# Two buffers for a tile's exponentials, one for the halves of z, in a fused attention and feed-forward kernel

## The chip, the cores and the metric

The kernel runs on one core of a Trainium2 chip. The metric is the device time of one execution in microseconds (us). Five engines work side by side, each through its own list of instructions in order: TensorE (PE in the profile; its weight loads are PEld), VectorE (DVE), ScalarE (ACT), GpSimd (POOL) and SyncE (SP), which here only issues DMAs. An instruction that waits holds up everything behind it on its engine, and a DMA that waits holds up the DMAs behind it on SP.

## The reference, cut to what matters

```python
k_p = k.reshape(B, H, Sp, 8, D).mean(axis=3)      # B = H = 8, S = 576, D = 64, Sp = 72
v_p = v.reshape(B, H, Sp, 8, D).mean(axis=3)
scores = scale * np.matmul(q, k_p.transpose(0, 1, 3, 2))
attn = np.exp(scores - np.max(scores, axis=-1, keepdims=True))
attn = attn / (np.sum(attn, axis=-1, keepdims=True) + 1e-09)
x = np.matmul(attn, v_p)                           # to (8, 576, 512)
xn = (x - mean(x)) / sqrt(var(x) + 1e-06) * g_ln
out = x + np.maximum(xn @ w_ch1, 0.0) @ w_ch2      # w_ch1: 512 x 2048, w_ch2: 2048 x 512
```

All inputs and the output are float32.

## The kernel before, in words

The 4608 tokens are cut into 36 tiles of 128 and 9 chunks of 4 tiles. Each tile passes two attention stages, each chunk one feed-forward stage. Values that need more than 16 bits are carried as two f16 parts, a high and a low one, and products are taken as three f16 matmuls.

**Scores and exponentials** (`stage_a`, token A; `scores` and `probs`). Four pairs of heads give scores in f32 into the PSUM tile `ps_s`, of which there is one (line 280). DVE takes the maximum (289) and writes the difference to `e` (290). ACT takes the exponential in place (299) and casts the high parts into `phl` (300, 303); POOL subtracts them from `e` for the low parts (307, 310). A DMA that transposes sends `phl` to `pt` (317). There are two `phl` tiles, taken in turn, and one `e`.

**Values and normalization** (`values`, token B). PE multiplies `pt` with the pooled v into `ps_x`, of which there is one (336, 337). DVE and ACT divide by the sum into `x` (340 to 357), DVE normalizes it to `z` (361 to 383), ACT casts the high part of z into the tile `hl` (387, called `zhl` in the code), POOL subtracts for the low part (388), and a transposing DMA sends `hl` to the chunk's `zT` (392). There is one `z`, and there are two `hl`.

**Feed-forward** (`ffn_in`, token I; `ffn_out`, token O). Line 411 multiplies w1 with `zT`, ACT and DVE write the result as two parts to a `ring` tile (419, 420), line 440 multiplies with w2, and DVE adds to `x` (450). A block of 512 columns is 12 matmuls in line 411, a tile of a half is 24 in line 440.

**Preparation.** k and v are loaded and pooled, mostly by POOL (216 to 232). The 16 weight blocks of 1 MB each are loaded as raw 64-bit words (155; the `raw` pool has two buffers), converted (`convert`: 164 and 176 on ACT, 167 and 168 on DVE), scaled and split in two (139 on ACT, 140 on DVE).

**What sets the order.** The string `START` lists the operations of chunks 0 and 1 with the loads, conversions and splits between them; a loop then interleaves chunk c with the attention stages of chunk c + 1. This is only the order in which the code is recorded. The framework's scheduler then orders each engine's list and decides when a tile of a pool is free, by a timing model of its own; a pool's number of buffers is one of its inputs. In `START` the first inputs of chunk 0 come as two halves of columns (`I.0.q.0`, `I.0.q.1`): the first half needs `zT` of tiles 0 and 1, the second that of tiles 2 and 3, and those of chunk 1 (`I.1.q`) need all of tiles 4 to 7.

Of the kernel before, what the change touches and what calls it, by code (L numbers as in the profile page):

```python
# [8 lines left out]
F32 = mybir.dt.float32  # L9
F16 = mybir.dt.float16  # L10
# [7 lines left out]
P = 128  # L18
B, H, S, D = 8, 8, 576, 64
POOL = 8  # L20
KV = S // POOL
KA, KR = 64, KV - 64
KB = KV + 2 * KR
DM = H * D
# [36 lines left out]
def attn_ffn_kernel(ctx: ExitStack, tc: tile.TileContext, qT, kT, v, g, w1, w2, out):  # L61
# [3 lines left out]
    wk1 = ctx.enter_context(tc.tile_pool(name="wk1", bufs=1))  # L65
    wk2 = ctx.enter_context(tc.tile_pool(name="wk2", bufs=2))
# [33 lines left out]
    def scalar_tile(name, n=1):  # L100
        return small.tile([P, n], F32, name=name)
# [155 lines left out]
    q_sb, E, PT, X, Z, zTs = {}, {}, {}, {}, {}, {}  # L257

    def segments(t):

        lo, res = t * P, []
        while lo < (t + 1) * P:
            b = lo // S
            hi = min((t + 1) * P, (b + 1) * S)
            res.append((slice(lo - t * P, hi - t * P), b))
            lo = hi
        return res
# [3 lines left out]
        nc.sync.dma_start(out=q_sb[t], in_=qT[t])  # L271

    def scores(t):
        E[t] = e = wk1.tile([P, H, KV], F32, name="e")
        q = q_sb.pop(t)
        mx = scalar_tile("mx", H)
        ps = ps_s.tile([P, 2, 512], F32, name="ps_s")
        for p in range(NPAIR):
            for r, b in segments(t):
                nc.tensor.matmul(  # L280
                    ps[r, p // 2, p % 2 * 2 * KV : (p % 2 + 1) * 2 * KV],
                    lhsT=q[:, p, r],
                    rhs=kblk[b % NKB][:, p, :],
                    start=True,
                    stop=True,
                )
        sc = ps[:, :, : 4 * KV].rearrange("p a (h k) -> p a h k", k=KV)
        mx = mx.rearrange("p (a h) -> p a h", a=2)
        nc.vector.tensor_reduce(out=mx, in_=sc, axis=AX.X, op=ALU.max)  # L289
        nc.vector.tensor_tensor(  # L290
            out=e.rearrange("p (a h) k -> p a h k", a=2),
            in0=sc,
            in1=mx.unsqueeze(3).broadcast_to([P, 2, 4, KV]),
            op=ALU.subtract,
        )
# [23 lines left out]
    def values(t):  # L319

        segs = segments(t)
        if len(segs) == 1:
            cv = CV[segs[0][1]]
        else:
            cv = scalar_tile("cvm")
            for r, b in segs:
                nc.vector.tensor_copy(out=cv[r], in_=CV[b][r])
        pt = PT.pop(t)
        sm, rs = scalar_tile("sm", H), scalar_tile("rs", H)
        X[t] = x = xres.tile([P, DM], F32, name="x")  # L330
        ps = ps_x.tile([P, 2, 512], F32, name="ps_x")
        px = ps[:, :, : H // 2 * (D + 1)].rearrange("p a (h d) -> p a h d", d=D + 1)
        for r, b in segs:
            for h in range(H):
                o = px[r, h // 4, h % 4]
                nc.tensor.matmul(o, lhsT=pt[:, h, r], rhs=VA[b][:, h, :], start=True, stop=False)  # L336
                nc.tensor.matmul(  # L337
                    o, lhsT=pt[:KB, H + h, r], rhs=VB[b][:, h, :], start=False, stop=True
                )
        nc.vector.tensor_scalar(  # L340
            out=sm.rearrange("p (a h) -> p a h", a=2),
            in0=px[:, :, :, D],
            scalar1=1e-9,
            scalar2=cv,
            op0=ALU.add,
            op1=ALU.mult,
        )
        nc.vector.reciprocal(out=rs, in_=sm)
        xh = x.rearrange("p (h d) -> p h d", d=D)
        nc.vector.tensor_tensor(  # L350
            out=xh[:, 0:4, :],
            in0=px[:, 0, :, 0:D],
            in1=rs[:, 0:4].unsqueeze(2).broadcast_to([P, 4, D]),
            op=ALU.mult,
        )
        for i in range(4):
            nc.scalar.activation(  # L357
                out=xh[:, 4 + i, :], in_=px[:, 1, i, 0:D], func=AF.Copy, scale=rs[:, 4 + i : 5 + i]
            )
        st, mv = scalar_tile("st", 6), scalar_tile("mv2", 2)  # L360
        nc.vector.bn_stats(out=st, in_=x)  # L361
        nc.vector.bn_aggr(out=mv, in_=st)
        ve, y, a = scalar_tile("ve"), scalar_tile("y"), scalar_tile("a")
        nc.vector.tensor_scalar(
            out=ve, in0=mv[:, 1:2], scalar1=1e-6, scalar2=Z_VAR, op0=ALU.add, op1=ALU.mult
        )
        nc.vector.tensor_scalar(
            out=y.bitcast(I32),
            in0=ve.bitcast(I32),
            scalar1=-0.5,  # L370
            scalar2=RSQRT_MAGIC,
            op0=ALU.mult,
            op1=ALU.add,
        )
        for _ in range(3):
            nc.vector.tensor_scalar(
                out=a, in0=y, scalar1=ve, scalar2=y, op0=ALU.mult, op1=ALU.mult
            )
            nc.vector.tensor_scalar(
                out=y, in0=a, scalar1=1.5, scalar2=y, op0=ALU.subtract, op1=ALU.mult  # L380
            )
        Z[t] = z = wk1.tile([P, DM], F32, name="z")
        nc.vector.tensor_scalar(  # L383
            out=z, in0=x, scalar1=mv[:, 0:1], scalar2=y, op0=ALU.subtract, op1=ALU.mult
        )
        zhl = wk2.tile([P, 2, DM], F16, name="hl")
        nc.scalar.copy(out=zhl[:, 0, :], in_=z)  # L387
        nc.gpsimd.tensor_tensor(out=zhl[:, 1, :], in0=z, in1=zhl[:, 0, :], op=ALU.subtract)  # L388
        c, tt = divmod(t, TPC)
        if tt == 0:  # L390
            zTs[c] = wk2.tile([P, 2 * NKT, CH], F16, name="zT")
        nc.sync.dma_start_transpose(
            out=zTs[c][:, :, tt * P : (tt + 1) * P], in_=zhl.rearrange("p a d -> p (a d)")
        )
# [62 lines left out]
    def stage_a(t):  # L457
        if t + 2 < NTT:
            load_q(t + 2)
        scores(t)  # L460
        probs(t)
# [53 lines left out]
    def out_half(c, h):  # L515
# [3 lines left out]
    ops = {  # L519
        "LD": first_loads, "K0": first_k, "V0": first_v, "R": load_raw,  # L520
        "Q": load_q, "A": stage_a, "B": values, "C": convert, "M1": max_w1, "M2": max_w2, "S": split_w,
        "I": in_quarter, "O": out_half, "HK": half_k, "HV": half_v,
    }
# [4 lines left out]
    for c in range(2, NRUN):  # L528
        units = []
        for h in range(2):  # L530
            units += [(ffn_in, c, f) for f in range(h * NFT // 2, (h + 1) * NFT // 2)]
            units += [(ffn_out, c, tt, h) for tt in range(TPC)]
        for u, (op, *args) in enumerate(units):
            if c + 1 < NRUN:
                if u in A_AT:
                    stage_a((c + 1) * TPC + A_AT.index(u))
                if u in B_AT:
                    t = (c + 1) * TPC + B_AT.index(u)
                    values(t)
                    b = t * P // S + 2  # L540
                    if b < B and (t + 1) * P >= (b - 1) * S:
                        prep_k(b)
                        prep_v(b)
            op(*args)
# [26 lines left out]
```

## Time and profile before

| | us |
|---|---|
| three runs | 899.89, 900.61, 900.71 |
| median | 900.61 |
| the profiled execution | 902.73 |
| its span in the profile | 900.6 |
| PE busy in the span | 830.0 (92%) |
| DVE, ACT, POOL busy | 427.9, 264.3, 261.8 |

The span runs from the first to the last recorded instruction of the profiled execution, which took 2.1 us more than its span and 2.1 us more than the median of the three runs. Matmuls overlap each other in the records, so a busy PE is not a PE at its peak. Times in the trace are counted from the start of the span.

### The profile page before, as it was taken

Reading aid. Unit: us, or ns where it says so; the run is one execution under the profiler, and the core shown is the slowest. Engines: PE = TensorE matmul, PEld = TensorE weight load, DVE = VectorE, ACT = ScalarE, POOL = GpSimd, SP = SyncE. Lnnn points to the kernel's source line nnn. Section 1 sums busy time; section 2 is a strip of 40 time slices with the busy share of each in tenths; the row PEclk is TensorE's granted clock in tenths of the full one; section 3 lists DMA queues with packets and bytes.
Section 4 is the critical chain, followed back from the end, with each engine's and each line's share of the span. In section 5 each row is a group of like instructions: output and inputs, shape, how many; then the busy total and the mean of one; then the engine's idle time right before and its main releaser. Section 6 shows DMA issues by size and latency. Waiting matters only on the chain.

```text
span 900.6 us, 11909 instructions
## 1 busy us (share of the span) xinstructions
PE 830.0 (92%) x4524; PEld 419.3 (47%) x4524; DVE 427.9 (48%) x986; ACT 264.3 (29%) x513; POOL 261.8 (29%) x414
## 2 busy tenths in 40 slices
PE   2246895999999999999999999999999999999998
PEld 1235743444444444454454544544544454444443
DVE  7687795335562643365335533653354335432121
ACT  2675673314131221233123312331232123211020
POOL 5684688205242150056002620230011002100000
PEclk9999996999999999999999999999999999999999
DMA  8989996102352322254223432332223121310001
GB/s 305 275 220 276 261 261 153 27 0 65 77 129 72 62 66 62 59 138 100 50 59 86 114 71 59 85 69 56 59 59 83 36 59 36 70 38 22 1 1 47
DMA packets 137289, 84.80 MB, mean 94 GB/s; under 512 B 116113, under 2 KB 117265, under 8 KB 135185
## 3 DMA queue, kind: packets, MB, share of 16 engines
q1 hardware_dynamic: 135696, 82.86, 36.1%
q10 hardware_dynamic: 1536, 1.20, 0.6%
q8 instruction: 35, 0.57, 0.3%
q14 instruction: 22, 0.17, 0.1%
HBM read 45.09 MB, written 9.44 MB: 61 GB/s over the span
## 4 chain that ended last, share of the span: by engine, by line
PE 80%; DMA 9%; POOL 5%; DVE 2%; ACT 1%; issue 1%; SPq 1%; ACTq 0%; POOLq 0%
PE ps_f L411 38%; PE ps_f L440 38%; DMA pt<-phl 3%; PE ps_s L280 2%; DMA kr<-in_kT_dram 2%; DMA q<-in_qT_dram 1%; PE ps_x L336 1%; PE ps_x L337 1%; POOL kr L216 1%; DMA raw<-in_w_dram 1%; DVE w L168 1%; DMA raw<-in_v_dram 1%; DMA va<-vh 1%; POOL vr L230 1%; POOL phl L307 1%
## 5 line engine op out<-in xcount | busy, mean ns | idle before, releaser
L411 PE MATMUL ps_f<-zT,w 128*128 128x512 f16 (+1 forms) x1824 | 387.9, 372 | 4.6 <-DMA zT<-hl 3.9
L440 PE MATMUL ps_f<-w,ring 128*128 128x512 f16 x1728 | 379.1, 379 | 0.0
L411 PEld LDWEIGHTS <-w 128*128 128x128 f16 x1824 | 179.4, 99 | 195.7 <-issue 5.3
L440 PEld LDWEIGHTS <-ring 128*128 128x128 f16 x1728 | 168.1, 98 | 199.3 <-issue 0.2
L419 ACT ACTIVATE ring<-ps_f 128x512 f16<-128x512 f32 (+1 forms) x152 | 86.9, 573 | 275.3 <-PE ps_f L411 256.5
L420 DVE SCALAR_TENSOR_TENSOR ring<-ps_f,ring 128x512 f16<-128x512 f32 (+1 forms) x152 | 99.9, 659 | 140.5 <-ACT ring L419 138.8
L450 DVE SCALAR_TENSOR_TENSOR x<-ps_f,c_out,x 128x512 f32<-128x512 f32 x72 | 53.9, 749 | 187.4 <-PE ps_f L440 187.4
L307 POOL TENSOR_TENSOR phl<-e,phl 128x512 f16<-128x512 f32 x36 | 43.8, 1216 | 261.3 <-ACT phl L300 248.7
L280 PE MATMUL ps_s<-kblk,q 128*128 128x144 f32 (+1 forms) x320 | 56.3, 342 | 44.4 <-issue 22.5
L388 POOL TENSOR_TENSOR hl<-z,hl 128x512 f16<-128x512 f32 x36 | 42.7, 1185 | 125.3 <-ACT hl L387 120.3
L280 PEld LDWEIGHTS ps_s<-kblk,q 128*128 128x128 f32 (+1 forms) x320 | 47.9, 215 | 53.0 <-issue 32.6
L299 ACT ACTIVATE e<-e 128x576 f32<-128x576 f32 x36 | 24.6, 683 | 163.6 <-DVE e L290 156.6
L357 ACT ACTIVATE x<-ps_x,rs 128x64 f32<-128x64 f32 x144 | 33.3, 313 | 74.5 <-DVE x L350 33.3
L230 POOL TENSOR_TENSOR vr<-vr 72x256 f32<-72x256 f32 x56 | 45.5, 819 | 26.7 <-DMA vr<-in_v_dram 26.3
L300 ACT CAST phl<-e 128x1024 f16<-128x1024 f32 x36 | 37.5, 1041 | 8.0 <-DMA pt<-phl 7.5
L387 ACT CAST hl<-z 128x512 f16<-128x512 f32 x36 | 22.2, 617 | 57.0 <-DVE z L383 55.4
L232 POOL TENSOR_TENSOR vp<-vr 72x64 f32<-72x64 f32 x56 | 21.8, 405 | 57.8 <-DVE vb L140 57.5
L336 PE MATMUL ps_x<-va,pt 128*128 128x65 f16 (+1 forms) x320 | 27.5, 200 | 9.7 <-DMA pt<-phl 6.4
L361 DVE BATCH_NORM_STATS2 st<-x 128x6 f32<-128x512 f32 x36 | 24.9, 691 | 24.2 <-ACT x L357 24.0
L216 POOL TENSOR_TENSOR kr<-kr 128x288 f32<-128x288 f32 x29 | 25.7, 892 | 26.8 <-DMA kr<-in_kT_dram 26.4
L289 DVE TENSOR_REDUCE mx<-ps_s 128x8 f32<-128x576 f32 x36 | 26.8, 745 | 9.2 <-PE ps_s L280 9.1
L220 POOL TENSOR_TENSOR kblk<-kr 64x72 f32<-64x72 f32 x58 | 21.7, 374 | 32.1 <-PE ps_s L280 29.2
(80 smaller groups left out, 474.7 us busy)
## 6 DMA issues: line engine op xcount, KB each, us to landing
raw<-in_w_dram SPq DMA_DIRECT2D x12, 1024.0 KB
q<-in_qT_dram SPq DMA_DIRECT2D x36, 256.0 KB
out_dram<-x SPq DMA_DIRECT2D x36, 256.0 KB
kr<-in_kT_dram SPq DMA_DIRECT2D x30, 288.0 KB
vr<-in_v_dram SPq DMA_DIRECT2D x56, 144.0 KB
ring<-in_w_dram SPq DMA_DIRECT2D x4, 1024.0 KB
raw<-in_v_dram SPq DMA_DIRECT2D x8, 144.0 KB
va<-vh ACTq DMA_DIRECT2D x16, 65.0 KB
```

The source lines that it names most:

```text
L216: eng.tensor_add(out=kr[:, 0:4, :], in0=kr[:, 0:4, :], in1=kr[:, 4:8, :])
L230: eng.tensor_add(out=vr[:, 0:4, :], in0=vr[:, 0:4, :], in1=vr[:, 4:8, :])
L280: nc.tensor.matmul(ps[r, p // 2, p % 2 * 2 * KV : (p % 2 + 1) * 2 * KV], lhsT=q[:, p, r], rhs=kblk[b % NKB][:, p, :], start=True, stop=True,)
L300: nc.scalar.copy(out=ph[:, :, :, 0:KA], in_=e[:, :, 0:KA].unsqueeze(1).broadcast_to([P, 2, H, KA]))
L307: nc.gpsimd.tensor_tensor(out=ph[:, 0, :, KA:P], in0=e[:, :, 0:KA], in1=ph[:, 0, :, 0:KA], op=ALU.subtract)
L336: nc.tensor.matmul(o, lhsT=pt[:, h, r], rhs=VA[b][:, h, :], start=True, stop=False)
L388: nc.gpsimd.tensor_tensor(out=zhl[:, 1, :], in0=z, in1=zhl[:, 0, :], op=ALU.subtract)
L411: nc.tensor.matmul(ps, lhsT=w[:, part, fs], rhs=zT[:, kz, cols], start=(n == 0), stop=(n == 3 * NKT - 1),)
L419: nc.scalar.activation(out=h[:, 0, i, cols], in_=ps, func=AF.Relu)
L420: nc.vector.scalar_tensor_tensor(out=h[:, 1, i, cols], in0=ps, scalar=0.0, in1=h[:, 0, i, cols], op0=ALU.max, op1=ALU.subtract,)
L440: nc.tensor.matmul(ps, lhsT=h[:, part, i, cols], rhs=w[:, wp, j], start=(n == 0), stop=(n == 3 * NFT // 2 - 1),)
L450: nc.vector.scalar_tensor_tensor(out=x, in0=ps, scalar=c_out[:, half : half + 1], in1=x, op0=ALU.mult, op1=ALU.add)
```

## The change

Two pools change hands. `e` comes from a pool of two buffers, so that the difference of the next tile can be written while the last reader of the tile before is not done. `hl` comes from a pool of one, so that the high part of the next z waits until the transposing DMA has read the one before.

```diff
     def scores(t):
-        E[t] = e = wk1.tile([P, H, KV], F32, name="e")
+        E[t] = e = wk2.tile([P, H, KV], F32, name="e")
...
-        zhl = wk2.tile([P, 2, DM], F16, name="hl")
+        zhl = wk1.tile([P, 2, DM], F16, name="hl")
         nc.scalar.copy(out=zhl[:, 0, :], in_=z)
         nc.gpsimd.tensor_tensor(out=zhl[:, 1, :], in0=z, in1=zhl[:, 0, :], op=ALU.subtract)
```

No instruction is added or taken away. The scheduler's order of chunks 0 and 1 is another one on every engine; from the inputs of chunk 2 on it differs in a few places, and from tile 16 on PE's list is the same.

First place: ACT, from the first conversions of w2 to the first values (`e_348` is tile 2, `e_388` tile 3, `x_223` the values of tile 0). Before:

```order
L139 ACTIVATE w1_88<-w1_88,gs_92 128x1024
L300 CAST phl0_104<-e_348 128x16x64
L303 CAST phl0_104<-e_348 128x8x16
L176 ACTIVATE raw_433,wm2_96<-w2_89 128x1024
L139 ACTIVATE w1_88<-w1_88,gs_92 128x1024
L357 ACTIVATE x_223<-ps_x_224,rs_222 128x64 x4
L299 ACTIVATE e_388<-e_388 128x576
L139 ACTIVATE w1_88<-w1_88,gs_92 128x1024
L300 CAST phl1_105<-e_388 128x16x64
```

After:

```order
L299 ACTIVATE e_388<-e_388 128x576
L176 ACTIVATE raw_404,wm2_96<-w2_89 128x1024
L164 ACTIVATE w2_89<-raw_433 128x1024
L139 ACTIVATE w1_88<-w1_88,gs_92 128x1024
L300 CAST phl0_104<-e_348 128x16x64
L303 CAST phl0_104<-e_348 128x8x16
L176 ACTIVATE raw_433,wm2_96<-w2_89 128x1024
L139 ACTIVATE w1_88<-w1_88,gs_92 128x1024
L300 CAST phl1_105<-e_388 128x16x64
```

The exponential of tile 3 has moved ahead of the casts of tile 2, which it could not do with one `e`, and its casts ahead of the values of tile 0.

Second place: SP, around the transposing DMAs of tile 3's `hl` (`hl_550`) and of tile 6's exponentials (`pt_910`); `pt_1042` is tile 7, `raw_1076` and `raw_1078` are the last two blocks of w1, `raw_1551` and `raw_1555` blocks 5 and 6 of w2. Before:

```order
L271 DMA q_1766<-in_qT_dram 128x512
L155 DMA raw_1070<-in_w1_dram 128x2048
L392 DMA_TRANSPOSE zT_268<-hl_550 128x8x128
L155 DMA raw_1076<-in_w1_dram 128x2048
L211 DMA kr_1695<-in_kT_dram 128x576
L317 DMA_TRANSPOSE pt_910<-phl0_104 128x16x128
L317 DMA_TRANSPOSE pt_1042<-phl1_105 128x16x128
L155 DMA raw_1078<-in_w1_dram 128x2048
```

After:

```order
L155 DMA raw_1078<-in_w1_dram 128x2048
L271 DMA q_1828<-in_qT_dram 128x512
L211 DMA kr_1971<-in_kT_dram 128x576
L155 DMA raw_1551<-in_w2_dram 128x2048
L317 DMA_TRANSPOSE pt_910<-phl0_104 128x16x128
L392 DMA_TRANSPOSE zT_268<-hl_550 128x8x128
L317 DMA_TRANSPOSE pt_1042<-phl1_105 128x16x128
L155 DMA raw_1555<-in_w2_dram 128x2048
```

Two more weight blocks (and three pieces of k, three of v and one q, counted from the start) now stand ahead of `pt_910`, and tile 3's `hl` stands behind it.

Third place: PE, where the inputs of chunk 1 begin (`ps_f_1299`, line 411). `ps_x_1704` are the values of tile 8, `ps_s_2506` and `ps_s_2665` the scores of tiles 12 and 13, `ps_f_1268` the last outputs of chunk 0. Before:

```order
L337 MATMUL ps_x_1704<-vb_586,pt_1640 128x65
L280 MATMUL ps_s_2506<-kblk0_102,q_1828 128x144 x4
L280 MATMUL ps_s_2665<-kblk0_102,q_2263 64x144
L280 MATMUL ps_s_2665<-kblk1_103,q_2263 64x144
L411 LDWEIGHTS w1_88
L411 MATMUL ps_f_1299<-zT_777,w1_88 128x512
```

After:

```order
L440 LDWEIGHTS ring_783
L440 MATMUL ps_f_1268<-w2_89,ring_783 128x512
L411 LDWEIGHTS w1_88
L411 MATMUL ps_f_1299<-zT_777,w1_88 128x512
L411 LDWEIGHTS w1_88
```

Before, the values of tile 8 and the scores of tiles 12 and 13 (the two rows of `ps_s_2665` four times over) stood between the last outputs of chunk 0 and the inputs of chunk 1. Now nothing does: tiles 8 and 12 have moved in among the outputs of chunk 0, tile 13 behind the inputs of chunk 1. Further up, the rest of the scores of tile 9, the scores of tile 10 and the values of tile 6 have moved ahead of the second half of columns of chunk 0; before, the list came to that half straight after the values of tile 5. The scores of tile 14 have moved from the outputs of chunk 1 to those of chunk 2.

## Rows read from the trace of the kernel before

**Rows 1.** The page's parts 1 and 2: busy time of each engine with its share of the span and its instructions; then the span in 40 slices of 22.5 us, each digit the busy tenths of a slice (PEclk: the granted clock in tenths of full speed).

```profile
PE 830.0 (92%) x4524; PEld 419.3 (47%) x4524; DVE 427.9 (48%) x986; ACT 264.3 (29%) x513; POOL 261.8 (29%) x414
...
PE   2246895999999999999999999999999999999998
...
PEclk9999996999999999999999999999999999999999
DMA  8989996102352322254223432332223121310001
```

**Rows 2.** Busy time by stretch: from:to and length in us, then for each engine the busy us and, in brackets, the instructions, then the granted clock as a share of 2.4 GHz, the share of the DMA engines and GB/s.

```profile
79.70:95.60 15.90, 15.21 (x131) 12.27 (x131) 10.64 (x26) 8.80 (x20) 7.54 (x12) 1.00 1.00 289
95.60:105.00 9.40, 6.28 (x74) 5.51 (x71) 7.93 (x22) 4.64 (x12) 6.29 (x11) 1.00 1.20 189
105.00:113.20 8.20, 8.20 (x64) 6.83 (x61) 6.34 (x19) 5.90 (x12) 4.11 (x6) 0.79 0.99 323
113.20:137.00 23.80, 23.05 (x139) 11.42 (x136) 23.80 (x45) 17.74 (x31) 21.55 (x27) 1.00 0.92 256
137.00:150.60 13.60, 4.36 (x29) 2.81 (x26) 8.83 (x21) 4.38 (x7) 13.00 (x22) 0.61 0.66 150
150.60:161.00 10.40, 10.40 (x42) 4.46 (x43) 1.70 (x3) 2.47 (x4) 6.89 (x15) 0.85 0.38 109
161.00:900.60 739.60, 734.82 (x3904) 353.45 (x3902) 308.15 (x711) 175.10 (x355) 146.60 (x236) 1.00 0.25 61
```

**Rows 3.** PE's timeline: start and length in us, line, operation, output and inputs, shape, count, and in brackets the idle time before it with what ended it.

```profile
79.72 9.46 PE L411 MATMUL ps_f<-zT,w 128*128 128x256 f16 x60 [2.27 <-DMA zT<-hl]
...
95.65 4.09 PE L411 MATMUL ps_f<-zT,w 128*128 128x256 f16 x36
...
104.48 0.20 PE L336 MATMUL ps_x<-va,pt 128*128 128x65 f16 x1 [3.12 <-DMA pt<-phl]
...
105.01 0.49 PE L280 MATMUL ps_s<-kblk,q 128*128 128x144 f32 x2
105.33 7.07 PE L411 MATMUL ps_f<-zT,w 128*128 128x256 f16 x48
112.24 1.15 PE L280 MATMUL ps_s<-kblk,q 128*128 128x144 f32 x8
...
120.25 16.35 PE L440 MATMUL ps_f<-w,ring 128*128 128x512 f16 x75
...
144.45 1.67 PE L280 MATMUL ps_s<-kblk,q 128*64 128x144 f32 x10 [6.27 <-issue]
...
150.58 9.66 PE L411 MATMUL ps_f<-zT,w 128*128 128x512 f16 x37 [1.64 <-DMA zT<-hl]
```

**Rows 4.** The view of waits from 40 to 150 us, of ACT and of DVE: who waited for whom, us in total, times, the longest.

```profile
ACT phl L300 <- DMA pt<-phl: 5.5, 4, 2.1
...
DVE e L290 <- POOL phl L310: 1.6, 3, 0.9
```

**Rows 5.** SP's timeline: start and length of the issue of the transposing DMAs, L392 for `hl` of tiles 1, 3 and 7, L317 for the exponentials of tiles 6 and 7.

```profile
73.30 1.32 SPq L392 DMA_TRANSPOSE zT<-hl  x1
...
90.90 1.25 SPq L392 DMA_TRANSPOSE zT<-hl  x1
...
93.35 10.44 SPq L317 DMA_TRANSPOSE pt<-phl  x2
...
147.48 1.24 SPq L392 DMA_TRANSPOSE zT<-hl  x1
```

**Rows 6.** Timelines of ACT, DVE and POOL: the casts of z of tiles 4 and 7 on ACT, tile 7's z on DVE, and its low part on POOL.

```profile
112.85 0.62 ACT L387 CAST hl<-z 128x512 f16<-128x512 f32 x1
...
142.85 0.62 ACT L387 CAST hl<-z 128x512 f16<-128x512 f32 x1 [2.95 <-DVE z L383]
...
142.18 0.64 DVE L383 TENSOR_SCALAR z<-x,mv,y 128x512 f32<-128x512 f32 x1
...
146.30 1.15 POOL L388 TENSOR_TENSOR hl<-z,hl 128x512 f16<-128x512 f32 x1
```

**Rows 7.** Groups of instructions over the span, different shapes apart: line, operation, shapes and count, then busy us, mean ns of one, and the idle time before them.

```profile
L450 DVE SCALAR_TENSOR_TENSOR x<-ps_f,c_out,x 128x512 f32<-128x512 f32 x72 | 53.9, 749 | 187.4 <-PE ps_f L440 187.4
...
L388 POOL TENSOR_TENSOR hl<-z,hl 128x512 f16<-128x512 f32 x36 | 42.7, 1185 | 125.3 <-ACT hl L387 120.3 <-PE ps_f L411 3.0 <-POOL phl L310 1.9
...
L290 DVE TENSOR_TENSOR e<-ps_s,mx 128x576 f32<-128x576 f32 x36 | 27.2, 755 | 2.9 <-POOL phl L310 2.1
L289 DVE TENSOR_REDUCE mx<-ps_s 128x8 f32<-128x576 f32 x36 | 26.8, 745 | 9.2 <-PE ps_s L280 9.1
...
L387 ACT CAST hl<-z 128x512 f16<-128x512 f32 x36 | 22.2, 617 | 57.0 <-DVE z L383 55.4 <-POOL phl L307 1.4
```

**Rows 8.** The chain that ended last: start, us, what.

```profile
147.48 3.05 DMA zT<-hl
...
175.54 18.99 PE ps_f L440 x88
...
686.45 1.13 PE ps_s L280 x16
```

## The prediction

> **What bounds the kernel now.** I read the page first. PE is busy for 92% of the span, but its digits are low in the first slices and fall to 5 once more in the seventh, where the granted clock falls too (PEclk 6) [rows 1]. Then the busy time by stretch: from 161.0 us to the end PE is busy for 734.82 of 739.60 us, all at full clock [rows 2]. There it works at a steady rate: 88 matmuls of line 440 in 18.99 us, 0.216 us each [rows 8]. So from the inputs of chunk 1 on (150.58 us [rows 3]) PE sets the end, and its list from there is nearly the same after the change. What can change is how early it gets there. I call that moment the start of chunk 1.
>
> Up to it the reader is to see waits of PE that do not belong to one engine. The first half of columns of chunk 0 starts at 79.72 us, when `zT` lands; the values of tile 6 wait 3.12 us for `pt`; from 105 to 137 us PE is full; then it stands for most of 13.6 us, last of all for tile 7's `zT` [rows 2, 3]. In these 137 us the DMA engines are near full (shares 0.92 to 1.20 in the stretches from 79.7 to 137), and DVE has no idle time at all from 113.2 to 137.0 (23.80 of 23.80) [rows 2].
>
> The chain into 150.58 is read backwards: the landing took 3.05 us from 147.48 [rows 8], POOL's low part began at 146.30, ACT's cast at 142.85 after a wait of 2.95 for z, and DVE reached z at 142.18 [rows 6], after the full stretch. So DVE's queue, and not a buffer, made tile 7 late.
>
> **The second `e`.** It removes two kinds of wait. Directly it frees DVE of the waits of line 290 for POOL's last reader: 1.6 us in three times [rows 4]. That is little, because what is late next is the other pool: ACT's cast into `phl` waits for the transposing DMA that reads it, 5.5 us in four times [rows 4], and `phl` still has two buffers. Indirectly it moves the scores of the early tiles forward, and with them loads and conversions. I cost the time to the first half of columns at nothing: one score tile is free earlier, but the lists of PE ask for tile 8 and three quarters of tile 9 before that half, and `zT` of tile 1 still comes off the same full DMA engines. What hides it are those DMAs; if they did not, it would be worth at most the 1.6 us of line 290 and the 2.27 us that PE waited for `zT` [rows 3], 3.9 together, and as much the other way if the loads moved forward delay tile 1's `zT`.
>
> **The order behind it: later second half of columns.** PE's list now has the values of tile 6 ahead of the second half of columns. Before, that half began at 95.65, and the values of tile 6 stood behind its first four blocks and began at 104.48 [rows 3]. Their DMA was issued at 93.35, ten microseconds for two of them [rows 5]. It now stands behind two more weight blocks of 1 MB. At 323 GB/s, the rate from 105.0 to 113.2 [rows 2], 1.049 MB takes 3.2 us, so two take 6.5. Bounds: 104.5 us, if these blocks only take the place of others that went later, and 111.0 if they come on top. I take 106, nearer to the low end: over all DMAs ahead of tile 7's `hl` there is just one piece of k more than before, so most of what moved forward no longer stands behind. `zT` of tile 3 follows in the queue directly; I put it at 108 for the chain below, and PE, which needs all of it only with the second half, at 106.
>
> From there PE still has in its list, up to the start of chunk 1:
>
> - the second half, 96 matmuls of 256 columns: 48 took 7.07 us at a clock of 0.79, 36 took 4.09 at full clock [rows 2, 3], so 7.1 + 48/36 x 4.09 = 12.5 us (the first 48 again slow, after a wait);
> - the values of tiles 7 and 8: 0.53 each, 104.48 to 105.01 [rows 3], 1.1 us;
> - the scores of tiles 11 and 12: 1.15 each [rows 3], 2.3 us;
> - the outputs of half 0, 96 matmuls at 16.35/75 = 0.218 us [rows 3], 20.9 us.
>
> Sum 36.8, and 106 + 36.8 = 142.8, say 143 us. This holds if the splits of w2 keep up, as they did before, when 75 of these matmuls ran without a wait [rows 3].
>
> **The gap that goes.** Before, the values of tile 8 and the scores of tiles 12 and 13 stood in the gap of 137.0 to 150.6; tile 13 alone waited 6.27 us there, behind the difference of tile 12 in DVE's full queue [rows 2, 3]. Now nothing stands there, and tile 7's z goes ahead of the four additions of line 450 in DVE's list. So the start of chunk 1 is the later of PE's 143 and of the landing of tile 7's `zT`.
>
> **The single `hl`.** Its cost is a chain. The cast of tile 4's z may start once tile 3's `hl` has been read, that of tile 5 once tile 4's has, and so on: four links from tile 3 to tile 7. A link is the cast (0.62), POOL (1.19) [rows 7], the issue and the landing. From cast to issue at least 0.62 + 1.19 = 1.8 us, and for tile 7 it was 147.48 - 142.85 = 4.6 [rows 5, 6]; from issue to landing 3.05 for tile 7 [rows 8], and 79.72 - 73.30 = 6.4 for tile 1 [rows 3, 5]. So a link takes 4.9 to 11.0 us, and the trace before has none, since tile 4's cast began at 112.85 [rows 6], over 20 us after tile 3's issue at 90.90 [rows 5]. Bounds for tile 7: 108 + 4 x 4.9 = 128 and 108 + 4 x 11.0 = 152. I take 7.7 per link, between the short one and the congested one, since DVE's and POOL's other work goes on beside it: 139 us. That is under 143, so PE's own list decides, by a little.
>
> The Trainium skill, in "Trainium Kernel Development and Optimization", section Best Practices, advises double buffers so that a DMA and the work overlap; `hl` is read by a DMA and loses its second. By that rule the chain of four links would be paid in full, and the time is the last rival's below; by the rows of tile 4 the second buffer mostly stood unused, and the sum is as above.
>
> **Behind the start of chunk 1.** Before, the stall left PE at a clock of 0.61 in the gap and 0.85 from 150.6 to 161.0 [rows 2]: the first 37 matmuls took 9.66 us [rows 3] instead of 37 x 0.216 = 8.0. Without a long stall 1.7 us come back. Tile 13's scores move behind the start: its 16 records take 1.1 us at full rate, as tile 31's did [rows 8]. The scores of tile 14 now come 14 us or so before their values instead of 100: cost between 0 and 3 us (the wait of 3.12 for `pt` is the nearest row [rows 3]); I take 0.6.
>
> **The sum.** Start of chunk 1: 150.6 - 143 = 7.6 earlier. Clock: 1.7. Against it 1.1 + 0.6. That is 7.6 us, and I keep 7.0 for small waits that the new order must make somewhere. The profiled execution took 902.73 us, 2.1 over its span of 900.6 and over the median 900.61. So it would take 895.7, and the median of new runs 900.6 - 7.0 = 893.6 us.
>
> **Rivals.**
>
> *DVE's queue decides as before (no change).* For it: 23.80 of 23.80 us busy, and z of tile 7 late by DVE alone [rows 2, 6]. The work ahead of that z is nearly the same after: four additions of 0.749 less, the two scores operations of tile 12 (0.745 and 0.755) more [rows 7], 1.5 us less in all. If DVE also idles as long as before ahead of it, the start of chunk 1 is 150.6 - 1.5 = 149.1; with 1.7 paid back for tiles 13 and 14, the time is 900.8. Against it: weight blocks are loaded earlier, so that conversions should fill DVE's idle time before 113 us (10.64 of 15.90 and 7.93 of 9.40 us were busy [rows 2]).
>
> *The order gains more.* Values of tile 6 at 104.5, as before, and a short chain: 141.3, so 9.3 earlier in place of 7.6: 892. It lies within the forecast's range.
>
> *The single `hl` decides (slower).* If the links take 11.0 us and tile 6 and tile 3 come at the late end, 111 and 113, tile 7's `zT` lands at 113 + 44 = 157. The start of chunk 1 is 6.4 later, the clock's loss stays, and tiles 13 and 14 cost 1.7: 908.7 us. It decides from links of (150.6 - 108)/4 = 10.7 us, or of 9.4 with tile 3 at 113. For it: ACT stands in its queue while a cast waits, and holds up splits and relus behind it. Against it: the slow landing was one of the most crowded moments.
>
> **How the numbers follow.** The forecast, with a start of chunk 1 between 138 and 147, has 0.62; its own range is 888 to 898. DVE's queue has 0.16, the single `hl` 0.16, and 0.06 is left for a wait behind the start of chunk 1 that I do not see (tile 14), slower by a few us. What a measurement can tell from no change is 0.2%, 1.8 us. Faster: 0.62 and a little of DVE's case, 0.64. Same: 0.14. Slower: 0.22. The range of 8 in 10 goes from 886 to 904: it takes in DVE's case, and the chain's up to links of about 10 us with tile 3 at 113.
>
> **What would show it.** Right: PE's values of tile 6 waiting for `pt` until about 106, the second half of columns behind them, outputs of half 0 ending near 143, and line 411's 512-column blocks starting at once, with no fall of the clock. DVE's rival would show as z of tile 7 near 141 after a full stretch. The chain's would show as ACT's casts (387) of tiles 4 to 7 waiting for DMA `zT`, and PE waiting for `zT` beyond 150. The forecast is wrong if chunk 1 starts outside 138 to 147, or if PE waits more than 3 us in sum behind it.

## The result, and the profile after

The change made the kernel slower. Four runs took 905.54 to 906.99 us, median 905.85; before took 899.55 to 900.71 in the same session, median 900.25. The ratio on record is 1.0056, with a 95% interval of 1.0034 to 1.0079 (the plain quotient of the two medians, 1.0062, lies inside it). The forecast was 893.6 us. The profiled execution took 905.81 us, its span is 904.0, 3.4 more than before's. The medians are 5.6 us apart; the profiles show less of it because before's profiled execution (902.73) lay 2.5 over its median and after's lay at its own.

The slices of the page, which answer to [rows 1]:

```profile
PE 829.4 (92%) x4524; PEld 419.2 (46%) x4524; DVE 427.5 (47%) x986; ACT 264.0 (29%) x513; POOL 260.7 (29%) x414
...
PE   2335589999999999999999999999999999999998
...
PEclk9999899999999999999999999999999999999999
```

Busy times are as before. The 5 in the seventh slice is gone, and the clock's 6 with it: the gap that the forecast wanted gone is gone. But PE's low slices reach one further, with a 5 and an 8 at the fifth and sixth. The stretches, in the columns of [rows 2]:

```profile
74.90:85.20 10.30, 3.85 (x15) 3.48 (x16) 10.12 (x19) 4.70 (x8) 6.56 (x11) 1.00 0.79 224
85.20:95.30 10.10, 7.26 (x50) 5.69 (x49) 3.35 (x9) 3.20 (x9) 8.02 (x14) 1.00 1.05 289
...
102.50:114.30 11.80, 3.72 (x58) 3.23 (x57) 10.61 (x31) 8.24 (x19) 8.53 (x17) 0.79 1.03 300
...
133.70:153.20 19.50, 19.50 (x91) 8.69 (x91) 11.40 (x25) 7.18 (x10) 16.47 (x23) 1.00 0.72 154
153.20:161.00 7.80, 7.80 (x38) 3.56 (x38) 2.13 (x3) 1.19 (x2) 0.00 (x0) 1.00 0.01 2
161.00:904.00 743.00, 738.53 (x3925) 354.80 (x3923) 310.52 (x713) 176.74 (x357) 154.64 (x248) 1.00 0.26 62
```

PE now stands before chunk 0 (3.85 us busy of 10.30) and again from 102.5 to 114.3 (3.72 of 11.80). From 133.7 on it is full and at full clock, straight into chunk 1. PE's timeline, as [rows 3]:

```profile
83.61 1.78 PE L280 MATMUL ps_s<-kblk,q 128*128 128x144 f32 x6 [6.38 <-DVE rowmax L105]
85.18 0.27 PE L127 MATMUL ps_f<-ident,rowmax 72*128 72x72 bf16 x1
85.25 7.21 PE L411 MATMUL ps_f<-zT,w 128*128 128x256 f16 x48
95.31 5.76 PE L411 MATMUL ps_f<-zT,w 128*128 128x256 f16 x36 [2.85 <-DVE ring L420]
...
102.55 0.22 PE L336 MATMUL ps_x<-va,pt 128*64 128x65 f16 x1
...
112.89 0.24 PE L336 MATMUL ps_x<-va,pt 128*128 128x65 f16 x1 [6.66 <-DMA pt<-phl]
...
114.31 6.33 PE L411 MATMUL ps_f<-zT,w 128*128 128x256 f16 x48 [0.37 <-DMA zT<-hl]
...
131.62 1.24 PE L440 MATMUL ps_f<-w,ring 128*128 128x512 f16 x5 [2.01 <-DVE w L140]
...
153.18 7.08 PE L411 MATMUL ps_f<-zT,w 128*128 128x512 f16 x32
```

The first half of columns begins at 85.25 instead of 79.72, the second at 114.31 (forecast 106), chunk 1 at 153.18 instead of 150.58 (forecast 143). From there to the end of the span it is 750.8 us, before 750.0. So the loss lies ahead of chunk 1, and most of the forecast's error in the 8.3 us by which the second half is late.

### The profile page after: what moved, and what is told of

Same layout as the page of the kernel before. It is cut to its first block, busy times and chain, and to the rows that moved or that the text cites. A ratio compares the mean times of both kernels' runs of the same rounds, so it can differ in the third digit from the quotient of the medians.

```text
span 904.0 us, 11921 instructions
## 1 busy us (share of the span) xinstructions
PE 829.4 (92%) x4524; PEld 419.2 (46%) x4524; DVE 427.5 (47%) x986; ACT 264.0 (29%) x513; POOL 260.7 (29%) x414
## 4 chain that ended last, share of the span: by engine, by line
PE 86%; DMA 6%; ACT 2%; POOL 2%; DVE 2%; SPq 1%; issue 0%; ACTq 0%
PE ps_f L440 41%; PE ps_f L411 40%; PE ps_s L280 3%; DMA q<-in_qT_dram 2%; DMA raw<-in_w_dram 1%; DMA pt<-phl 1%; PE ps_x L336 1%; PE ps_x L337 1%; DMA raw<-in_v_dram 1%; ACT w L164 1%; DVE w L168 1%; POOL vr L230 1%; ACT phl L300 0%; POOL phl L307 0%; ACT raw L176 0%
## 5 line engine op out<-in xcount | busy, mean ns | idle before, releaser
L230 POOL TENSOR_TENSOR vr<-vr 72x256 f32<-72x256 f32 x56 | 42.9, 772 | 24.7 <-DMA vr<-in_v_dram 24.3
L220 POOL TENSOR_TENSOR kblk<-kr 64x72 f32<-64x72 f32 x58 | 22.5, 388 | 82.9 <-PE ps_s L280 80.1
L336 PEld LDWEIGHTS <-pt 128*128 128x128 f16 (+1 forms) x320 | 24.6, 106 | 15.4 <-DMA pt<-phl 7.5
L383 DVE TENSOR_SCALAR z<-x,mv,y 128x512 f32<-128x512 f32 x36 | 30.3, 842 | 2.6
```

The lines of the kernel that those rows point to most:

```text
L230: eng.tensor_add(out=vr[:, 0:4, :], in0=vr[:, 0:4, :], in1=vr[:, 4:8, :])
```

## Where the second half was lost: reading backwards

The values of tile 6 waited 6.66 us for `pt`. SP's timeline shows its issue:

```profile
96.60 0.36 SPq L211 DMA_DIRECT2D kr<-in_kT_dram  x1
101.30 0.35 SPq L155 DMA_DIRECT2D raw<-in_w_dram  x1
101.75 0.38 SPq L271 DMA_DIRECT2D q<-in_qT_dram  x1
102.22 0.38 SPq L211 DMA_DIRECT2D kr<-in_kT_dram  x1
103.21 0.33 SPq L155 DMA_DIRECT2D raw<-in_w_dram  x1
103.63 7.17 SPq L317 DMA_TRANSPOSE pt<-phl  x1
110.89 1.25 SPq L392 DMA_TRANSPOSE zT<-hl  x1
```

The two raw blocks of the forecast stand ahead of it. But the tile's exponentials go to `pt`, of which there are two (line 316 takes it from the pool of two), and tile 6's takes the place of tile 4's. Those are read by the values of tile 4, whose second part ran from 102.55 to 103.2; 0.4 us later the DMA went. The raw block just ahead of it went no sooner: it was issued at 103.21, when ACT had read the block that stood in its buffer before (line 176, in ACT's timeline):

```profile
102.98 0.20 ACT L176 ACTIVATION_READ_ACCUMULATOR raw<-w 128x1 f32 x1
```

So the queue and the buffer held `pt` to the same moment. Its issue then held SP for 7.17 us, and `zT` of tile 3 behind it. Two views could thus be the cause, the raw blocks in SP's queue and the place of tile 4's values on PE, where they now stand behind the last block of the first half instead of in its middle.

Those values also need `va` and `vb` of batch 1, which ACT issues, and here ACT's timeline shows a second loss:

```profile
87.54 0.50 ACTq L253 DMA_DIRECT2D va<-vh  x1
88.35 0.70 ACTq L254 DMA_DIRECT2D vb<-vh  x1
89.64 0.49 ACTq L253 DMA_DIRECT2D va<-vh  x1
93.69 0.68 ACTq L254 DMA_DIRECT2D vb<-vh  x1
94.41 0.94 ACT L419 ACTIVATE ring<-ps_f 128x256 f16<-128x256 f32 x3 [6.90 <-DMA vb<-vh]
```

The relus of the first blocks stood behind these four issues, and PE ran out of `ps_f` (2.85 us). In before the four went between 78.07 and 85.4 us, and PE, whose first half began at 79.72, ran 60 matmuls without a wait [rows 3]. They are late because the pooled v of batch 1 is: POOL finished it at 78.5 instead of 71.0, with pieces of k of batch 2 and low parts of later tiles ahead of it, and its maximum then came to PE (line 127) at 85.18 instead of 74.10, behind DVE's queue and tile 9's scores.

My first theory (Q) was SP's queue, as in the prediction; the second (R) ACT's; a third (T), after the first runs, the two `pt`. Over them stands the question whether the buffers (H) or only the order that the scheduler made for them (O) cost the time.

## The experiments

The order of an engine can be written down and pinned. A function at the end of the kernel reads a table of each list and adds, from each instruction to the next, an edge that carries no wait but that the scheduler must respect:

```diff
         attn_ffn_kernel(tc, *args)
+        pin_order(tc, nc)
```

So one list can be run on other buffers, or with one row moved. Each run is compared with before in the same session (before's medians went from 899.87 to 902.67 between sessions), so ratios are compared. Positions in traces of one order differ by up to 3.5 us (the first half began at 78.83, 80.34 and 82.28 us in three runs whose lists agree up to there), so distances count more than times.

### The buffers without their order, and half of the change

**old_order**: after's buffers, all five lists as in before.

> The buffers of after (two e, one hl), with every engine's list pinned to the order of before, instruction by instruction. Theory O (the order costs the time, the buffers themselves nothing): chunk 1 starts within 1 us of the 150.58 us of before, time 900.3 +- 1.5. Theory H (the single hl itself holds things up): casts of z or issues of zT wait, chunk 1 starts at 153 or later, time 903 to 908.

Ratio 0.9989 (0.9969 to 1.0010): no change. Chunk 1 began at 148.68, 1.9 ahead of before's 150.58: outside the 1 us expected, inside the 3.5 us by which traces of one order differ. The two buffer changes together cost nothing that can be measured. The single `hl` does make waits: the view of waits of ACT in this run has

```profile
ACT hl L387 <- DMA zT<-hl: 14.3, 3, 6.6
```

14.3 us in three casts, and none of it reaches the end. In after's own order no cast waits for `zT` at all. H is out, unless the second `e` gained what the single `hl` lost.

**one_hl**: half of the change, scheduled freely.

```diff
-        zhl = wk2.tile([P, 2, DM], F16, name="hl")
+        zhl = wk1.tile([P, 2, DM], F16, name="hl")
```

> Only the hl half of the change: one e as before, one hl; the scheduler orders it anew. Theory O expects no particular time, because this is a third order: between 896 and 908. If the single hl is what moves the time through the scheduler, 904 to 907, as the whole change; if the second e is, 899 to 902, as before.

Ratio 0.9958 (0.9938 to 0.9978), faster than before: within what O allowed, outside of both attributions. Chunk 1 begins at 144.86, close to the 143 that I had forecast for after, which is chance: it is another order. So giving up a buffer led the scheduler to a better order, and the second `e` on top of it to a worse one.

**order_of_one_hl**: that order on after's buffers, all five lists pinned.

> The buffers of after (two e, one hl), with every engine's list pinned to the order that the scheduler made for one_hl (one e, one hl). Theory O (a second e costs nothing by itself, only through the order that it leads the scheduler to): chunk 1 within 1.5 us of the 144.9 us of one_hl, ratio to before 0.994 to 0.998. Rival (the second e itself costs time): ratio 1.000 or more.

Ratio 0.9945 (0.9930 to 0.9960). The same change that costs 0.56% in the scheduler's order gains 0.55% in this one. That settles O against the rival. With the same lists and only `e` changed, one_hl and order_of_one_hl gave 0.9958 and 0.9945, with intervals that overlap: the second `e` is worth little by itself, which leaves little for it to have hidden in old_order. (The mirror image, after's order with one `e`, is not possible: there the exponential of tile 3 goes ahead of the casts of tile 2.)

### Which step of after's order is at fault

**act_relus_first**: on ACT only, in after's order.

```diff
-L253 DMA va_585<-vh_584
-L254 DMA vb_586<-vh_584
-L253 DMA va_585<-vh_584
-L254 DMA vb_586<-vh_584
 L419 ACTIVATE ring_648 (first to third block)
 L164 ACTIVATE w1_88<-raw_1070
 L419 ACTIVATE ring_648 (fourth block)
+L253 DMA va_585<-vh_584
+L254 DMA vb_586<-vh_584
+L253 DMA va_585<-vh_584
+L254 DMA vb_586<-vh_584
```

> After, pinned to its own order, with one move on ACT alone: the four va/vb DMAs of batch 1 go behind the first four relus of chunk 0's first half. Theory R (ACT's queue behind these DMAs stops PE by 2.85 us and makes raw buffers free late): the wait of 2.85 us for ring goes, raw of w1's last block is issued about 2 us before 101.3, second half of columns 1 to 3 us before 114.3, time 903 to 905. Rival: the second half waits for pt and zT that hang on other things, time 905.8 unchanged within 0.7.

Ratio 1.0022 (1.0004 to 1.0041), in place of 1.0056. PE's wait for `ring` is gone, 84 matmuls run on end:

```profile
83.45 10.27 PE L411 MATMUL ps_f<-zT,w 128*128 128x256 f16 x84
...
111.30 7.72 PE L411 MATMUL ps_f<-zT,w 128*128 128x256 f16 x48 [0.28 <-DMA zT<-hl]
...
150.70 9.66 PE L411 MATMUL ps_f<-zT,w 128*128 128x512 f16 x44
```

R holds in kind; its size is less sure. Between the ratios lie some 3 us, but the intervals overlap. In the trace the first half begins 1.80 sooner than in after, ahead of the DMAs that were moved, so that part is not the edit's; from there to the second half it is 27.85 us instead of 29.06, and to chunk 1 67.25 instead of 67.93. ACT's queue is worth 1 to 3 us. What PE still waits for is `va` (2.2 us, values of tile 4) and `pt` (5.6).

**sp_early**: on SP only, in after's order.

```diff
+L317 DMA_TRANSPOSE pt_910<-phl0_104
 L155 DMA raw_1078<-in_w1_dram
 L271 DMA q_1828<-in_qT_dram
 L211 DMA kr_1971<-in_kT_dram
+L392 DMA_TRANSPOSE zT_268<-hl_550
 L155 DMA raw_1551<-in_w2_dram
-L317 DMA_TRANSPOSE pt_910<-phl0_104
-L392 DMA_TRANSPOSE zT_268<-hl_550
```

> After, pinned to its own order, with two moves on SP alone: the pt DMA of tile 6 goes ahead of w1's last raw block, the zT DMA of tile 3 ahead of the next w2 block. Theory Q (the raw loads ahead of pt of tile 6 make the second half of columns late): pt issued near 97 instead of 103.6, landed by 106, second half of columns at 108 to 110 instead of 114.3, chunk 1 at 148 to 150 instead of 153.2, time 901 to 903. Rival: the raw blocks are needed as soon as that, and their conversion becomes late instead: time 905 to 908.

Q falls as the cause by itself. First in its queue, `pt` of tile 6 was still issued only at 102.57, just after the values of tile 4 (their last matmul began at 102.3). Meanwhile w1's last raw block stood behind it, was issued at 104.68, and ACT, in whose list its conversion stands ahead of the values' x, waited:

```profile
110.50 1.16 ACT L164 ACTIVATE w<-raw 128x1024 f32<-128x1024 f32 x1 [5.70 <-DMA raw<-in_w_dram]
...
114.05 0.92 ACT L357 ACTIVATE x<-ps_x,rs 128x64 f32<-128x64 f32 x4
```

Until 114 nobody had read tile 5's `ps_x`, and PE waited 9.5 us for it. Second half at 115.87, ratio 1.0046 (1.0029 to 1.0064), not told from after's.

**tile4_early** and **tile4_zt3_early**: the same with the values of tile 4 earlier on PE, and then with tile 3's `hl` earlier on ACT, POOL and SP too.

```diff
 L411 MATMUL ps_f_694 x12
+L336, L337 MATMUL ps_x_717 (second part, 16)
 L411 MATMUL ps_f_784 x12
...
 L411 MATMUL ps_f_829 x12
-L336, L337 MATMUL ps_x_717 (second part, 16)
```

> After, pinned to its own order, with the values of tile 4 moved on PE from behind the first half's block f7 to ahead of f4, and the two SP moves of the run sp_early. Theory T (pt has two buffers, so the pt DMA of tile 6 can only go once the values of tile 4 have been read, and their place on PE makes it late): pt of tile 6 issued at 96 to 98 instead of 103.6, second half of columns at 107 to 110 instead of 114.3, chunk 1 at 146 to 149, ratio to before 0.999 to 1.002. Rival (something else holds pt or zT of tile 3 as late): second half at 113 or later, ratio 1.004 or more, as sp_early.

> As tile4_early, and in addition tile 3's hl earlier: its cast on ACT goes ahead of the fourth relu, its low part on POOL ahead of the pooling of four pieces of k, its zT DMA on SP ahead of w1's last raw block. Theory T: both things that the second half needs are then there by 106, as the forecast had it: second half at 104 to 107, chunk 1 at 143 to 146, ratio 0.995 to 0.999. Rival (PE's 37 us from there to chunk 1 do not hold when it begins earlier, because the splits of w2 or DVE's queue are late): second half early, but chunk 1 at 148 or later.

Ratios 1.0071 (1.0046 to 1.0097) and 1.0068 (1.0041 to 1.0095): both miss. Half of T is seen: the values' last matmul began at 99.5 and 100.9, `pt` was issued at 99.78 and 101.21. But the values had to wait for `va` first (5.2 and 6.6 us), with blocks f4 to f7 behind them; in tile4_early w1's last raw block was issued at 105.47 (after: 101.30), since ACT read the buffer that it waits for only until 105.45, behind the relus of these late blocks, so that the x of tile 5 was late again (4.8 us); and the second half began at 116.01 and 116.61. Fixing the order at its end does not help while batch 1's v is late at its beginning.

**tile4_late**: the other way round, the fault put into the good order: in order_of_one_hl the rest of tile 4's values (15 matmuls) goes behind f7.

> order_of_one_hl with one move on PE alone: the rest of the values of tile 4 goes from amid the first half's block f6 to behind f7, where after has it. Theory T (the pt DMA of tile 6 waits for the values of tile 4 to free one of the two pt buffers): pt of tile 6 is issued within 1 us of the end of those values, at 96 to 98 instead of 94.0; second half of columns 0 to 3 us later than 103.3, chunk 1 at 146 to 149, ratio 0.995 to 0.999. Rival (the place in SP's queue decides): pt of tile 6 stays at 94 to 95.

The last of those values began at 100.7 and `pt` was issued at 100.94. Later than forecast in itself, since this run began its first half at 82.28, 3.5 us after order_of_one_hl; the link is the 0.2 us. Second half 26.2 us behind the first half, 24.5 in order_of_one_hl: 1.8 later, as expected. Chunk 1 began at 151.92, outside the 146 to 149 expected, in an execution 5.0 us above this run's median; from the first half it is 69.6 us, in order_of_one_hl 67.1. Ratio 0.9972 (0.9950 to 0.9994), 0.27% up, with intervals that just overlap. In 11 of the 14 traces `pt` of tile 6 was issued within 0.7 us of the start of the last matmul that read tile 4's; in the other three a DMA ahead of it on SP came between. T holds for this link.

**pool_pinned**: after's buffers, POOL's list alone pinned to that of one_hl; the scheduler makes the rest.

> The buffers of after (two e, one hl); only POOL's list is pinned, to the order it has in one_hl, and the scheduler orders the other engines anew around it. Theory V (in after POOL pools batch 1's v about 9 us later than in the good order, behind pieces of k, and the va/vb DMAs, the values of tile 4, pt of tile 6 and the second half of columns follow as late): the first va/vb DMA at 76 to 80 instead of 87.5, pt of tile 6 issued at 93 to 98, chunk 1 at 145 to 150, ratio to before 0.993 to 1.000. Rival (POOL's order is only one of several faults): chunk 1 at 152 or later, ratio 1.004 or more.

Ratio 1.0062 (1.0045 to 1.0078): the rival is right. The first `va` DMA came at 80.17 and the second half at 103.99, ten us sooner than in after, so far V holds. But `pt` of tile 6 (99.21, expected by 98) stood behind `zT` of tile 3 on SP, and before chunk 1 PE stands again as it did in before:

```profile
146.09 0.47 PE L280 MATMUL ps_s<-kblk,q 128*64 128x144 f32 x4 [2.09 <-POOL kblk L220]
148.70 0.75 PE L280 MATMUL ps_s<-kblk,q 128*64 128x144 f32 x4 [2.14 <-POOL kblk L220]
152.81 12.55 PE L411 MATMUL ps_f<-zT,w 128*128 128x512 f16 x45 [3.37 <-issue]
```

Tile 7's `zT` was issued at 149.59. An early second half without an early tile 7 is worth nothing.

### A version that beats both

In order_of_one_hl DVE is busy for 38.47 of the 40 us from 100 to 140. The conversions of w2's blocks 5 to 7 in that stretch are for half 1 and not needed until later.

**one_hl_w2_later** put them straight behind tile 7's z.

> one_hl, pinned to its own order, with the conversions of w2's blocks 5 to 7 moved behind z of tile 7 on DVE and ACT, the load of the last one behind its zT DMA on SP. Theory D (the full DVE queue from 100 to 140 us now sets both PE's waits and tile 7's zT): chunk 1 at 140 to 143 instead of 144.9, ratio to before 0.990 to 0.994. Rival (PE's own list decides): chunk 1 at 144 to 146, ratio 0.995 to 0.997; if the late conversions hold up the splits that half 1 needs, PE waits behind 160 us and the ratio is above 0.998.

A mistake of mine: the fourth split of w2 stood behind that z, and so behind conversions whose raw block is loaded after tile 7's `zT`. PE waited 16.78 us for it; ratio 1.0119 (1.0092 to 1.0146).

**w2_later** puts them in between the first blocks of chunk 1, on after's buffers; **w2_later_old_buffers** runs the same lists on before's.

```diff
 L420 SCALAR_TENSOR_TENSOR ring_1298<-ps_f_1299 (chunk 1, first block)
+L167 TENSOR_SCALAR raw_1551
+L168 SCALAR_TENSOR_TENSOR w2_89<-w2_89,raw_1551
```

> order_of_one_hl with the conversions of w2's blocks 5 to 7 moved on DVE and ACT in between the first blocks of chunk 1, behind the fourth split of w2 and the additions (in one_hl_w2_later they stood ahead of that split), the load of block 7 behind tile 7's zT DMA. Theory D (DVE's full queue makes tile 7's zT and the splits late): chunk 1 at 141 to 144 instead of 145.9, ratio 0.990 to 0.993. Rival (PE's list alone): 145 to 146, ratio 0.994 to 0.996; if a late conversion stops PE behind 160 us, above 0.997.

> The order of w2_later, on the buffers of before (one e, two hl). Theory O (the buffers count only through the order): within 0.3% of w2_later, so a ratio to before between 0.989 and 0.994, chunk 1 within 1.5 us of its 143.4. If the second e or the single hl is worth something once the order is good: a ratio outside that, above 0.994 or below 0.989.

Ratios 0.9914 (0.9884 to 0.9943) and 0.9917 (0.9904 to 0.9931). D's forecast is met, with chunk 1 at 143.38; from the second half to chunk 1 it is 38.4 us instead of 42.6, and DVE is no longer full (the edit takes work off ACT in that stretch too, which no run took apart):

```profile
100.00:140.00 40.00, 34.16 (x244) 23.13 (x245) 38.47 (x86) 28.67 (x53) 25.48 (x28) 0.91 0.95 240
```

```profile
100.00:140.00 40.00, 36.53 (x260) 24.37 (x261) 33.37 (x87) 24.49 (x50) 24.92 (x35) 0.91 0.97 233
```

(order_of_one_hl above, w2_later below; PE, PEld, DVE, ACT, POOL.) In w2_later_old_buffers chunk 1 began at 139.82, 3.6 before w2_later's, outside the 1.5 expected; 2.9 of it stand already at the first half (77.46 against 80.34), the rest I did not follow up, since the ratios agree. This order is 0.83 to 0.86% faster than before with either set of buffers.

## Why the prediction was wrong

The table holds three traces: before; after; and order_of_one_hl, which has after's buffers. Times in us.

| | before | after | good order |
|---|---|---|---|
| batch 1's v pooled | 71.0 | 78.5 | 69.6 |
| its maximum on PE (line 127) | 74.10 | 85.18 | 72.80 |
| fourth va/vb issue ends | 85.4 | 94.4 | 86.0 |
| last matmul of tile 4's values | 91.9 | 103.1 | 93.8 |
| `pt` of tile 6 issued | 93.35 | 103.63 | 94.04 |
| values of tile 6 | 104.48 | 112.89 | 102.38 |
| second half of columns | 95.65 | 114.31 | 103.28 |
| tile 7's `zT` issued | 147.48 | 149.46 | 142.40 |
| chunk 1 | 150.58 | 153.18 | 145.89 |

From v to the second half, after is 8 to 12 us behind the good order all the way down.

- **What bounds the kernel: right.** In all fourteen traces chunk 1 lies 749.7 to 751.9 us ahead of the end of the span. The start of chunk 1 is the time.
- **The first half costed at nothing: wrong.** It came 5.5 us later, beyond the bound of 3.9. I looked at `zT` of tile 1 and the DMAs. Of what else stands ahead of that half on PE I named three quarters of tile 9's scores and put no wait on them, but they waited 6.38 us for DVE's queue; the maximum of batch 1's v I did not name. DVE was busy for 10.12 of 10.30 us there.
- **The failed step: "Later second half of columns".** I put the values of tile 6 at 106, with bounds from 104.5 to 111.0, by counting bytes ahead of `pt` in SP's queue. Measured were 112.9. What the queue cost was not bytes: the raw block ahead waited until 103.2 for ACT to read its buffer, and with that block out of the way `pt` still went only behind tile 4's values (sp_early), because it waits for its own buffer (tile4_late). Those values stood on PE behind the whole first half, which began 5.5 us late and then stood 2.85 us for relus behind the `va` and `vb` issues (act_relus_first: 1 to 3 us by ACT alone); moved ahead, they waited for `va` itself (tile4_early), which POOL's and ACT's order had made late. Both moves, batch 1's v and tile 4's values, were in the lists of POOL and PE; I named neither. No single move in after's order brought back more than 3 us, so how the loss divides among these links is not shown.
- **36.8 us from there to chunk 1: right but for a wait.** 38.9 were measured, 2.0 of the difference at line 440 for a split of w2.
- **The gap goes and the clock comes back: right.** Nothing stands ahead of chunk 1, and PE is full, at 1.00, from 133.7 us. Tiles 13 and 14 and the clock were to cancel; the 750.8 instead of 750.0 says they nearly did.
- **The single `hl` does not decide: right,** and the rival that gave it the slower side is refuted (old_order, order_of_one_hl). The slower side came by a mechanism that I had not listed. Its number was off, though, and this step failed too: tile 7's `zT` was issued at 149.46, not there at 139, because POOL took 4.6 us to come to its low part behind k, v and a later tile's low part (cast 143.71, low part 148.28) and z itself was late. With before's landing of 3.05, even a PE at 143 would have waited some 9 us for it, and pool_pinned shows that case: the second half at 103.99, tile 7's `zT` at 149.59, chunk 1 at 152.81. I checked that chain for `hl` and left the queues of DVE and POOL out of it. The advice in the Trainium skill, "Trainium Kernel Development and Optimization", section Best Practices, to double-buffer for overlap is not borne out for this tile: in one good order the kernel runs as fast with one `hl` and two `e` as with two `hl` and one `e` (0.9914 and 0.9917).

What stays open: why the scheduler rates after's order above the others is not in any trace. And the halves were taken apart on one side only: the second `e` alone, with two `hl`, was not run.

## What to carry to other kernels

Where a scheduler orders the lists, a change of buffers is a change of order first: pin the old order on the new buffers, and the new order on the old ones where that is possible, before a buffer is blamed or praised. When a DMA looks late, ask which earlier reader frees its target, as well as what stands ahead of it in its queue and what that waits for: here both held it to the same moment, and taking one away gained nothing. And a start that needs two things is as late as the later one: follow both chains through every engine's queue before a gain is put on either.

## What the runs showed of the hardware

Issuing a DMA can hold the issuing engine's queue far longer than the 0.35 us of the plain loads above: the DMA for `pt` of tile 6 held SP for 7.17 us in after and for 2.02 in sp_early, and in after 4.0 us lie between the starts of ACT's third and fourth `va`/`vb` issue. What sets these lengths is not shown.

DVE's z (line 383) took 0.53 us in some places and 3.66 in another, with the same shape. The long one in order_of_one_hl, in DVE's timeline, and the busy times in just this stretch (PE, PEld, DVE, ACT, POOL):

```profile
134.63 3.66 DVE L383 TENSOR_SCALAR z<-x,mv,y 128x512 f32<-128x512 f32 x1
```

```profile
134.63:138.29 3.66, 3.66 (x18) 1.67 (x17) 3.66 (x2) 0.08 (x1) 3.66 (x7) 1.00 0.54 118
```

POOL was busy in all of these 3.66 us, and in all of the 2.47 that another z took in after. The Trainium skill says in "Advanced Engine Details and Errata", section VectorE Performance Modes, that VectorE's second SBUF port is shared with GpSimd, and that GpSimd's instructions and VectorE's in a mode with two read ports interfere or block each other; the long rows fit that, though no row shows in which mode z ran. A busy POOL does not always bring a long z, as another of the same run shows:

```profile
71.10 0.53 DVE L383 TENSOR_SCALAR z<-x,mv,y 128x512 f32<-128x512 f32 x1
```

```profile
71.10:71.63 0.53, 0.00 (x0) 0.00 (x0) 0.53 (x3) 0.53 (x4) 0.53 (x1) 1.00 1.12 203
```

In the fourteen traces together, the 166 z beside an idle POOL took 0.49 to 0.55 us; of the 219 beside a POOL that was busy throughout, 152 took over 1 us and 35 under 0.6. No run took POOL's work away from beside a long one. In the prediction I took DVE's operations at their mean lengths.
